# A fused attention and gated-feed-forward block: all q/k projections ahead of the gates, a planner that counts exponentials, maxima in steps of their own, even head sets

## The chip, the core and the metric

The kernel runs on one core of a Trainium2 chip. The core has a matrix engine (TensorE, PE), a vector engine (VectorE, DVE), an activation engine (ScalarE, ACT), a general engine (GpSimd, POOL), a queue that only issues transfers (SyncE, SP), and DMA engines between HBM and the on-chip memory. PE writes its results to the banks of PSUM, from which DVE and ACT read them. Each engine works through its own list of instructions in order; semaphores hold an instruction back until what it needs is there.

The metric is the device time of one launch in microseconds (us), the median of several runs. One launch was also recorded by the hardware profiler; the profile and the trace come from it.

## The reference

For `x` of 2048 rows and 576 columns (S = 2048, D = 576), 32 heads of width 18, and a feed-forward width of 4608:

```python
xn = layernorm(x)
q, k, v = split(xn @ wqkv)                       # 32 heads of width 18
p = softmax(q @ k.T * 18 ** -0.5)                # per head, 2048 x 2048
s = concat_heads(p @ v) @ wo
g = silu((gelu(xn @ w_gate) * (xn @ w_up)) @ w_down)
out = x + s * g
```

All data are float32. The kernel splits most operands into a high and a low float16 part and forms three products for one, so that the result stays near float32.

## The kernel before, in words

**Projections.** After the layer norm, the normalised rows stand transposed on the chip as a high and a low half (XHT, XL). The weights are taken in *units*: `v`, five *j units* (the q and k columns of one set of heads, `j0` to `j4`), eighteen *c units* (256 columns of `w_gate` and `w_up`, and the matching 256 rows of `w_down`), and `wo`. `prep` (L210) lays down what a unit's weights need: loads on SP's queue, maxima for a power-of-two scale, a round trip through HBM that spreads the maximum, then the split into a high half (ACT, L359) and a low half (POOL, L366 and L367, or one DVE instruction). These pieces wait in a background list, `bg`; `subtick` (L151) takes some of them when the room it is given allows it. `Rest` and `Gate` items hold the list back for a time or until a condition holds.

`v` and `j0` are projected near the start. The other 22 units form one stream, the **gate stream** (`order`, L1094 on; `pairs`, L1130 on). Its grain is a *pair*: 27 *slots* in two halves of 14 and 13, each slot two matmuls side by side on half the rows of the array (L517). A j unit has four pairs, a c unit eight; 4320 slots in all. Between the two halves of a pair, another product must have used PE (`g_run`, L1165). In the order before, the j units stand between the c units: j1, j2 (its pairs dealt out alternately with c0's), c1, c2, j3, c3, c4, j4, and then the rest.

A pair of a j unit is evacuated by ACT and DVE and stored to HBM (`evac_j`). A pair of a c unit goes through the gelu: evacuations on ACT, five products on POOL, a tanh on ACT, two more products on POOL, and a split into `hhi` and `hlo`. Two such pairs make a block, whose second half, when it is finished, queues eight *down stages* (`DownPair`, L792): the product with `w_down`, 12 matmuls a stage (L816). Every second stage is *late*: DVE then adds the result to `y` (L836).

**Attention.** Heads go in 16 *head pairs*. For a head pair, first the row maxima of the scores are needed: `qk1` (L1409) makes scores into one two-bank tile, and DVE reduces it (L1417). `max_end` (L1421) turns the 128 x 32 maxima into two rows that are appended to Q: a reduction (L1430), three POOL operations, a transpose (L1437), a DMA to HBM, and DMAs from there into QT (L1444). Then `qk2` (L1465) makes scores again, transposed and with the maximum taken off, ACT takes the exponential (L1475; L1477 and L1478 where the two heads lie in different sets, as each set has its own scale), and a *burst* multiplies three or four exponentials by V (L1494), which DVE adds up (L1502). `norm` divides and stores to OHL.

**The steps.** The main loop (from L1775 on) has 64 steps for each head pair. A step issues `qk2` for this head pair, `qk1` for the next one (from step 58 on, for the one after it), and then, as a plan says, a down stage or none and some slots of the gate stream. The last step of a gate pair holds the burst and no slots. The plan for one gate pair is made by `make_plan`: it tries all numbers of steps near a due size (`size`: steps left over pairs left) and all ways of putting down stages on them, spreads the slots by `spread`, and takes the layout with the least cost. The cost is the time that `lost` works out, plus terms for the distance from the due size and from the wanted number of down stages (`want`), plus others. A shortfall of down stages is carried into the next plan without a bound (`frac[1]`).

**Start and end.** Before the loop, 64 steps make the maxima of head pair 0 while `v` and then the gate stream fill PE (L1611 on); seven more steps then begin head pair 1. When the gate stream is over, the output products (`OutPair`) begin, which load OHL (`load_ohl`); the first call of that load stands in the step that finds the stream finished.

Of the kernel before, what the change touches and what calls it, by code (L numbers as in the profile page):

```python
# [24 lines left out]
NJ = 5  # L25
CF = 256
# [68 lines left out]
def kernel(ctx: ExitStack, tc: tile.TileContext, x, wqkv, wo, w_gate, w_up, w_down, out):  # L95
# [114 lines left out]
    def prep(name, parts, n, down=None, urgent=False, free=None, dfree=None, lead=1, vec=(), spare=False, early=False, slow=1.0):  # L210
# [139 lines left out]
        def split_hi(t):  # L350
            if t == 0:
                if spare == "P":
# [41 lines left out]
        act, dve = on_act(), on_dve()  # L394
        low_cost = [dve if t in vec else on_pool(2.75) for t in range(5)]
# [155 lines left out]
    def heads_of(j):  # L551
        return list(range(7 * j, min(7 * j + 7, H)))
# [72 lines left out]
    def spec_j(j):  # L625
        n = DH * len(heads_of(j))
        return f"j{j}", [(wqkv, 126 * j), (wqkv, D + 126 * j)], n
# [479 lines left out]
    def make_prep(i, **how):  # L1107
        kind, spec = order[i]
        w, pieces = prep(
            *spec, free=lambda: done_units[0] >= {2: 0, 3: 1}.get(i, i - 1),  # L1110
            dfree=lambda: kind[1] < 2 or dndone[kind[1] - 2] == NT,
            lead=1, vec=(1, 3) if i == 4 else (), **how,
        )
        preps[i] = w
        return pieces
# [14 lines left out]
    def pairs():  # L1130
# [5 lines left out]
        yield from unit(1)  # L1136
        ahead = [unit(2), unit(3)]
# [5 lines left out]
        for i in range(4, len(order) - 1):  # L1143
# [247 lines left out]
    def load_qk(p):  # L1391
        q = ap.tile([P, S], F16, tag="QT", name=f"QT{p}", bufs=3)
        k = ap.tile([P, S], F16, tag="KT", name=f"KT{p}", bufs=3)
        for h in range(2):
            j, hl = divmod(2 * p + h, 7)
# [25 lines left out]
    def max_end(p):  # L1421
# [3 lines left out]
        def a():  # L1425
            gp = nc.gpsimd
            defer.spend(on_pool(1.0))
            mx = sm.tile([P, 2, NT], F32, tag="rmx", name=f"rmx{p}", bufs=2)
            mc = st["mc"] = sm.tile([P, 2, 2, NT], F16, tag="rmc", name=f"rmc{p}", bufs=2)
            nc.vector.tensor_reduce(mx, PM[p], op=ALU.max, axis=AX.X, negate=True)  # L1430
# [9 lines left out]

        def c():
# [23 lines left out]
    def qk2(p, qb, kt, tag):  # L1465
# [7 lines left out]
        j0, j1 = (2 * p) // 7, (2 * p + 1) // 7  # L1473
# [123 lines left out]
    pj2, pc0 = make_prep(2, spare="P", early=True), make_prep(3, early=True, slow=1.5)  # L1597
    for p in (pj2, pc0):
        p.pop(0)[1]()

    def until_gate(p):
        n = next(k for k, f in enumerate(p) if isinstance(f, Gate))
        return p[:n], p[n:]

    pj2, sj2 = until_gate(pj2)
    pc0, sc0 = until_gate(pc0)
    bg.append(Rest(14.0))
    bg.extend(pj1 + pc0[:1] + pj2[:6] + pc0[2:10] + pj2[6:10] + pc0[11:12] + pj2[10:] + sj2 + pc0[13:] + sc0)
    fills(11, 2.0)
    k = 0  # L1610
    while k < 64:  # L1611
        if k == 12:
            load_qk(1)
        if done_units[0]:
# [4 lines left out]
            qk1(0, k)  # L1619
            subtick(FIRST)  # L1620
            g_run(7)
            subtick({"A": 0.75, "V": 0.3, "T": 0.5})
            k += 1
        else:
            qk1(0, k)
            qk1(0, k + 1)
            side = 0.0
            for _ in range(2):
                subtick(FIRST)
                side += FIRST["V"] - defer.room["V"]  # L1630
            fill(2.03 + side)
            k += 2
# [5 lines left out]
    for k in range(AHEAD + 1):  # L1638
# [4 lines left out]
        g_run(7)  # L1643
        subtick(dict(FIRST, T=1.75))
# [8 lines left out]
    ROW_MAX, EVAC, ADD, TOUCH = 1.28, 0.86, 0.75, 0.0  # L1653
# [22 lines left out]
    def lost(steps):  # L1676

        t = vec = red = 0.0
        ideal = 0.0
# [279 lines left out]
```

## Time and profile before

| | |
|---|---|
| median of 3 runs (lowest, highest) | 2538.12 us (2537.28, 2538.24) |
| the profiled execution | 2540.97 us |
| its span, first to last instruction | 2539.1 us |
| granted TensorE clock, mean | 0.998 |
| row maxima, L1417, DVE | 1250.9 us, 1024 of 1224 ns |
| exponentials, L1475, ACT | 995.2 us, 896 of 1112 ns |
| exponentials in halves, L1477 and L1478, ACT | 87.8 and 87.2 us, 128 of each |
| addition to `y`, L836, DVE | 219.8 us, 272 of 808 ns |

A row of the timeline reads: start in us from the beginning of the span, duration in us, engine, line of the kernel, operation, output <- inputs, shapes, how many of them, and in brackets how long the engine had been idle before and what ended that. A row of the windows has the stretch, its length, and for each engine the busy time in it with the number of instructions in brackets, then the granted clock, the DMA share and GB/s; when it is asked for one line, only that line's instructions are counted. A row of the groups has line, engine, operation, tiles, shapes and count, then busy us and the mean ns of one, then the idle time ahead of them. Times of one line on PE add up to more than its share, as neighbouring matmuls overlap.

### The profile page before, as it was taken

What the parts mean: (1) busy time and instruction counts of PE and PEld (TensorE: products, weight loads), DVE (VectorE), ACT (ScalarE), POOL (GpSimd) and SP (SyncE); (2) the same over time, 40 slices, a digit from 0 to 9 for tenths busy, and PEclk for the clock granted to TensorE, in tenths of its full rate; (3) what the DMA queues carried; (4) which work ended last, traced back from release to release, by engine and by line L of the source; (5) the groups of instructions that cost most, each with busy time, mean ns of one, the idle gap of its engine ahead of it and who ended that gap; (6) DMA issues with size and microseconds to landing.
All of it is one profiled execution on the core that took longest, in us unless ns stands there. A gap on an engine that the chain in (4) does not pass through costs nothing.

```text
span 2539.1 us, 61428 instructions
## 1 busy us (share of the span) xinstructions
PE 2490.0 (98%) x26216; PEld 1297.5 (51%) x26216; DVE 1837.8 (72%) x2108; ACT 1657.1 (65%) x2066; POOL 1542.0 (61%) x1587
## 2 busy tenths in 40 slices
PE   7999999999999999999999999999999999999898
PEld 6864544554445444445445444454444454544455
DVE  7587777787768777777777777776777777777444
ACT  6236676667776767666767676677766666666574
POOL 3367575547655476766757585857676767666413
PEclk9999999999999999999999999999999999999999
DMA  5631110221011210201111120101010111010124
GB/s 161 163 121 51 28 24 6 59 88 25 19 52 30 68 44 6 58 10 53 26 27 40 25 57 11 53 16 50 16 45 19 38 24 44 25 35 8 41 64 141
DMA packets 139689, 118.71 MB, mean 47 GB/s; under 512 B 64810, under 2 KB 118832, under 8 KB 139417
## 3 DMA queue, kind: packets, MB, share of 16 engines
q1 hardware_dynamic: 136553, 106.92, 15.4%
q0 software_dynamic: 1568, 5.37, 0.8%
q8 instruction: 206, 3.38, 0.6%
q10 hardware_dynamic: 1296, 2.51, 0.3%
q14 instruction: 66, 0.54, 0.1%
HBM read 84.89 MB, written 29.61 MB: 45 GB/s over the span
## 4 chain that ended last, share of the span: by engine, by line
PE 90%; DVE 5%; ACT 2%; DMA 1%; issue 1%; SPq 0%; POOL 0%; POOLq 0%; ACTq 0%; DVEq 0%
PE ma_t L517 17%; PE mb_t L517 16%; PE md_t L816 16%; PE md_t L1494 10%; PE s L1469 10%; PE s L1414 9%; PE ma_t L1494 8%; DVE PM L1417 1%; ACT P L1475 1%; PE md_t L998 1%; PE mb_t L998 1%; ACT P L1477 1%; PE pv_t L665 1%; PE ma_t L998 1%; PE ma_t L665 0%
## 5 line engine op out<-in xcount | busy, mean ns | idle before, releaser
L1417 DVE TENSOR_REDUCE PM<-s 128x2 f32<-128x1024 f32 x1024 | 1250.9, 1224 | 350.3 <-PE s L1414 343.2
L1475 ACT ACTIVATE P<-s,etab 128x1024 f32<-128x1024 f32 x896 | 995.2, 1112 | 590.3 <-PE s L1469 581.7
L517 PE MATMUL ma_t<-XHT,whi_c 64*128 64x512 f16 x1440 | 541.2, 376 | 0.5 <-DVE osb L1500 0.3
L517 PE MATMUL mb_t<-XHT,whi_c 64*128 64x512 f16 x1440 | 541.2, 376 | 0.2 <-ACT gv L722 0.2
L517 PE MATMUL ma_t<-XHT,wlo_c 64*128 64x512 f16 x1296 | 486.5, 375 | 0.0
L517 PE MATMUL mb_t<-XHT,wlo_c 64*128 64x512 f16 x1152 | 432.4, 375 | 0.0
L517 PE MATMUL ma_t<-XL,whi_c 64*128 64x512 f16 x1152 | 432.3, 375 | 0.0
L517 PE MATMUL mb_t<-XL,whi_c 64*128 64x512 f16 x1152 | 432.3, 375 | 0.0
L1469 PE MATMUL s<-QT,KT 56*128 56x512 f16 x2048 | 403.0, 380 | 4.4 <-DMA QT<-md 1.2
L1414 PE MATMUL s<-KT,QT 54*128 54x512 f16 x2048 | 396.7, 377 | 3.3 <-DVE PM L1417 2.6
L517 PEld LDWEIGHTS <-whi_c 64*128 64x128 f16 x5184 | 273.1, 94 | 216.6 <-issue 3.2
L816 PE MATMUL md_t<-dhi_c,hhi 64*128 64x288 f16 x2304 | 334.9, 283 | 1.9 <-DVE osb L1500 0.8
L816 PE MATMUL md_t<-dhi_c,hlo 64*128 64x288 f16 x2304 | 334.5, 283 | 0.0
L816 PE MATMUL md_t<-dlo_c,hhi 64*128 64x288 f16 x2304 | 334.1, 282 | 0.0
L752 POOL TENSOR_SCALAR tw<-tw 128x512 f32<-128x512 f32 x144 | 90.2, 626 | 376.2 <-ACT tw L744 376.1
L816 PEld LDWEIGHTS <-hhi 64*128 64x128 f16 x4608 | 237.7, 94 | 150.6 <-issue 10.7
L777 POOL TENSOR_TENSOR hlo<-gv,hhi 128x512 f16<-128x512 f32 x144 | 167.8, 1165 | 222.6 <-ACT hhi L770 219.7
L1494 PE MATMUL md_t<-P,VT 128*32 128x512 f32 x2296 | 267.2, 596 | 1.2 <-issue 0.9
L1469 PEld LDWEIGHTS <-KT 56*128 56x128 f16 x2048 | 123.8, 94 | 256.6 <-issue 166.9
L836 DVE SCALAR_TENSOR_TENSOR y<-md_t,c_c,y 128x576 f32<-128x576 f32 x272 | 219.8, 808 | 18.6 <-PE md_t L816 18.6
L1494 PE MATMUL ma_t<-P,VT 128*32 128x512 f32 x1712 | 200.2, 596 | 0.7 <-DVE ob L1040 0.4
L517 PEld LDWEIGHTS <-wlo_c 64*128 64x128 f16 x2592 | 136.7, 94 | 119.8
(255 smaller groups left out, 4062.0 us busy)
## 6 DMA issues: line engine op xcount, KB each, us to landing
draw_c<-in_B_w_down SPq DMA_DIRECT2D x18, 576.0 KB
raw_c<-in_B_w_gate SPq DMA_DIRECT2D x18, 512.0 KB
raw_c<-in_B_w_up SPq DMA_DIRECT2D x18, 512.0 KB
obr<-rd SPq DMA_DIRECT2D x30, 256.0 KB
KT<-KD SPq DMA_DIRECT2D x32, 224.0 KB
QT<-QD SPq DMA_DIRECT2D x32, 216.0 KB
VS<-vst POOLq DMA_DIRECT2D x16, 304.0 KB, 5.8
VT<-VS SPq DMA_DIRECT2D x16, 304.0 KB
```

The lines of the kernel that those rows point to most:

```text
L517: m = nc.tensor.matmul(o, lw, xx, start=self.stage == 0 and self.k == 0, stop=self.stage == 1 and self.k == self.slots - 1, skip_group_che ...
L665: self.last = nc.tensor.matmul(self.m[hf].t[:, 0:288], a, b, start=not second and k == 0, stop=bool(second) and k == n - 1, skip_group_che ...
L752: gp.tensor_scalar(st["t"], st["t"], 1.0, 1.0, op0=ALU.mult, op1=ALU.add)
L777: gp.tensor_tensor(hs.lo[:, ft], st["v"], hs.hi[:, ft], op=ALU.subtract)
L816: m = nc.tensor.matmul(self.t.t[:, hf, 0:288], a[r, ft, sl], b[r, ft, 288 * hf:288 * hf + 288], start=self.stage == 0 and k == 0, stop=sel ...
L836: nc.vector.scalar_tensor_tensor(yy, y, w.c, yy, op0=ALU.mult, op1=ALU.add)
L998: m = nc.tensor.matmul(o, a, b, start=self.stage == 0 and self.k == 0, stop=self.stage == 1 and self.k == len(terms) - 1, skip_group_check ...
L1414: nc.tensor.matmul(s1[:, h], QT[p][r, P * qt:P * qt + P], KT[p][r, 512 * kb:512 * kb + 512], start=True, stop=True)
L1417: nc.vector.tensor_reduce(PM[p][:, :, qt, kb:kb + 1], s1, op=ALU.max, axis=AX.X)
L1469: nc.tensor.matmul(s2[:, h], KT[p][r, P * kt:P * kt + P], QT[p][r, 512 * qb:512 * qb + 512], start=True, stop=True)
L1475: nc.scalar.activation(pt, s2, AF.Exp, scale=ETAB[j0])
L1494: nc.tensor.matmul(t.t[qd:qd + 32, :], VT[p][:, c0:c0 + 32], pt[:, h], start=kt == k0, stop=kt == k1, skip_group_check=True,)
```

## The change

Six things are done.

1. The head sets have 6, 6, 6, 7 and 7 heads (`HEADS`) where they had 7, 7, 7, 7 and 4.
2. In the gate stream all j units stand ahead of the c units; j4's pairs are dealt out alternately with c0's. The preparation of j2, j3, j4 and c0 is put into the background list before the start, in a new order by hand. `home` says where a unit's split weights live: those of j2 and j3 take buffers of the exponentials ("P").
3. In the start, the number of slots in a step follows a target (`g_round`): 540 slots by the end of it.
4. `lost` works with a chain for each of PE, DVE and ACT: the row maximum, the exponential (1.113, or 1.4 where a head pair straddles sets), the late evacuation.
5. `make_plan` wants at least four down stages in a pair, weighs the distance from the wanted number and from the due size more, bounds what is carried over, and improves the twelve best layouts by moving single slots inside a half.
6. `max_end` forms the two parts of the maximum by two DVE operations in place of three on POOL, and its three parts are issued ahead of steps 58, 59 and 60; before, the first came behind step 57 and the others behind step 60.

```diff
+HEADS = [0, 6, 12, 18, 25, 32]
...
     def heads_of(j):
-        return list(range(7 * j, min(7 * j + 7, H)))
+        return list(range(HEADS[j], HEADS[j + 1]))
...
-    for k, j in enumerate(units_j):
-        order += [j] + [units_c.pop(0) for _ in range((0, 3, 2, 2)[k])]
-    order += units_c
+    order += units_j + units_c
...
-            *spec, free=lambda: done_units[0] >= {2: 0, 3: 1}.get(i, i - 1),
+            *spec, free=lambda: done_units[0] >= {2: 0, 3: 0, 4: 1, 5: 2}.get(i, i - 1),
...
         def a():
-            gp = nc.gpsimd
-            defer.spend(on_pool(1.0))
-            mx = sm.tile([P, 2, NT], F32, tag="rmx", name=f"rmx{p}", bufs=2)
+            mx = st["mx"] = sm.tile([P, 2, NT], F32, tag="rmx", name=f"rmx{p}", bufs=2)
+            nc.vector.tensor_reduce(mx, PM[p], op=ALU.max, axis=AX.X, negate=True)
+
+        def b():
+            mx = st["mx"]
             mc = st["mc"] = sm.tile([P, 2, 2, NT], F16, tag="rmc", name=f"rmc{p}", bufs=2)
-            nc.vector.tensor_reduce(mx, PM[p], op=ALU.max, axis=AX.X, negate=True)
-            gp.tensor_scalar(mx, mx, 2.0 ** -15, None, op0=ALU.mult)
-            gp.tensor_scalar(mc[:, :, 0], mx, 1.0, None, op0=ALU.mult)
-            gp.tensor_tensor(mc[:, :, 1], mx, mc[:, :, 0], op=ALU.subtract)
-
-        def b():
+            nc.vector.tensor_scalar(mc[:, :, 0], mx, 2.0 ** -15, None, op0=ALU.mult)
+            nc.vector.scalar_tensor_tensor(
+                mc[:, :, 1], mx, 2.0 ** -15, mc[:, :, 0], op0=ALU.mult, op1=ALU.subtract
+            )
+
+        def c():
             st["mt"] = sm.tile([P, 64], F16, tag="rms", name=f"rms{p}", bufs=1)
             nc.vector.transpose(st["mt"], st["mc"].rearrange("p a b c -> p (a b c)"))
             st["md"] = dp.tile([P, 64], F16, tag="md", name=f"md{p}", bufs=2)
             nc.sync.dma_start(st["md"], st["mt"])
-
-        def c():
             md = st["md"]
...
+    pj2, pj3, pj4 = (make_prep(k, spare="P", home="P" if k < 4 else None, early=True) for k in (2, 3, 4))
+    pc0 = make_prep(5, early=True)
...
+    bg.extend(pj1 + pc0[:1] + [lj3] + pj2[:8] + pj3[:6] + pj2[9:13] + pj3[7:8] + pj2[13:])
+    bg.extend([lj4] + pj3[9:] + pj4[:6] + pc0[2:5] + pj4[7:8] + pc0[5:9] + pj4[9:13] + pc0[9:10])
+    bg.extend(pj4[13:19] + pc0[11:12] + pj4[19:] + [Rest(2.5)] + pc0[13:])
...
+    START = 20 * 27
+
+    def g_round(target):
+        n = g_left()
+        if gs.all - gs.left + n > target + 4:
+            n = (n + 1) // 2
+        room = 0.75 if n < 10 else 1.5
+        subtick({"A": room, "V": room, "T": 0.12 + 0.1 * n})
+        g_run(n)
+        subtick({"A": room, "V": 0.3, "T": 0.1 + 0.1 * n})
...
-            subtick(FIRST)
-            g_run(7)
-            subtick({"A": 0.75, "V": 0.3, "T": 0.5})
-            k += 1
+            g_round(START * (k + 1 - k0) / (70 - k0))
...
+    def lost(steps, exp):
+
+        t = ideal = ex = red = y = 0.0
+        vec = 0.83
         for d, g, late, first in steps:
-            t1 = max(t + 0.21, red + 0.055)
-            e1 = t1 + 0.22
-            vec = red = max(vec, e1 + 0.16) + ROW_MAX - 0.05
-            w = d * D_STAGE + (BURST if g is None else g * G_SLOT)
+            q = max(t, ex + 0.055)
+            t1 = max(q + 0.22, red + 0.055)
+            ex = max(ex - 0.1, q + 0.48) + exp
+            vec = red = max(vec - 0.085, t1 + 0.42) + 1.226
+            t = t1 + 0.21
             if d:
-                vec = max(vec, e1 + D_STAGE) + (EVAC if late else TOUCH)
-            t = e1 + w
-            if g is None:
-                vec = max(vec, t) + ADD
-            elif first:
-                vec = max(vec, t) + TOUCH
-            ideal += BLOCK + w
-        return max(t, red + 0.055 - 0.21) - ideal
+                t = (t if late else max(t, y + 0.055)) + D_STAGE
+                if late:
+                    vec = y = max(vec - 0.085, t + 0.1) + 0.808
+            t += BURST if g is None else g * G_SLOT
+            ideal += BLOCK + d * D_STAGE + (BURST if g is None else g * G_SLOT)
+        return max(t, red + 0.055 - 0.22, ex + 0.055) - ideal
...
-        want = min(8.0, dleft[0] / pairs + frac[1])
+        want = min(8.0, max(4.0, (dleft[0] - 16) / pairs) + frac[1])
...
-                    cost = lost(seq) + busy * ds[-1] + held_a * (not ds[0]) + 0.3 * abs(n - size) + 0.15 * abs(sum(ds) - want) + 0.02 * (max(works) - min(works))
+                    fixed = busy * ds[-1] + held_a * (not ds[0]) + 0.3 * abs(n - size) + 0.15 * (n - size) ** 2 + 0.25 * abs(sum(ds) - want)
+                    found.append((lost(seq, exp) + fixed + 0.02 * (max(works) - min(works)), fixed, seq, m))
...
-        frac[1] = want - sum(d for d, _, _, _ in seq)
+        frac[1] = max(-0.3, min(0.3, want - sum(d for d, _, _, _ in seq)))
...
+            if more and 0 <= i - 64 + AHEAD < 3:
+                if i == 64 - AHEAD:
+                    steps = max_end(p + 1)
+                steps[i - 64 + AHEAD]()
...
-            if more and i == 60:
-                steps[1]()
-                steps[2]()
-            if more and i == 57:
-                steps = max_end(p + 1)
-                steps[0]()
```

More of the change, by code (lines that the diff above doesn't have):

```diff
@@ L208, with prep @@
         pass
-    def prep(name, parts, n, down=None, urgent=False, free=None, dfree=None, lead=1, vec=(), spare=False, early=False, slow=1.0):
+    def prep(name, parts, n, down=None, urgent=False, free=None, dfree=None, lead=1, vec=(), spare=False, home=None, early=False, slow=1.0):
         w = W()
@@ L392, in rest @@
                 pieces.append(Rest(span))
-        act, dve = on_act(), on_dve()
-        low_cost = [dve if t in vec else on_pool(2.75) for t in range(5)]
+        act, dve = on_act(), on_dve(0.7 if n > P else 0.42)
+        low_cost = [dve if t in vec else on_pool(2.75 if n > P else 1.65) for t in range(5)]
         if not early:
@@ L551, in heads_of, with set_of @@
     def heads_of(j):
-        return list(range(7 * j, min(7 * j + 7, H)))
+        return list(range(HEADS[j], HEADS[j + 1]))
+    def set_of(h):
+        j = max(j for j in range(NJ) if HEADS[j] <= h)
+        return j, h - HEADS[j]
     jdone = {}
@@ L1134, in unit @@
             done_units[0] += 1
-        yield from unit(1)
-        ahead = [unit(2), unit(3)]
+        for i in range(1, NJ - 1):
+            yield from unit(i)
+        ahead = [unit(NJ - 1), unit(NJ)]
         yield next(ahead[0])
@@ L1142, in pairs @@
         yield from ahead[1]
-        for i in range(4, len(order) - 1):
+        for i in range(NJ + 1, len(order) - 1):
             yield from unit(i)
@@ L1613 @@
             load_qk(1)
+        qk1(0, k)
         if done_units[0]:
@@ L1618 @@
                 banks.remove(("mc", "pv"))
-            qk1(0, k)
-            subtick(FIRST)
-            g_run(7)
-            subtick({"A": 0.75, "V": 0.3, "T": 0.5})
-            k += 1
-        else:
[L1625 to L1632, printed above, removed]
+            g_round(START * (k + 1 - k0) / (70 - k0))
+        else:
+            subtick({"A": 0.9, "V": 0.9, "T": 2.1})
+            fill(1.9)
+            k0 = k + 1
+        k += 1
     load_v(0)
```

59 lines of the change are left out of this document (35 added, 24 removed).

## The prediction

> **What bounds the kernel now.** I read the page's busy times first, then the timeline of the TensorE (PE), then windows of single lines, then the waits of VectorE (DVE), and the end of the run last.
>
> ```profile
> PE 2490.0 (98%) x26216; PEld 1297.5 (51%) x26216; DVE 1837.8 (72%) x2108; ACT 1657.1 (65%) x2066; POOL 1542.0 (61%) x1587
> ```
>
> PE has work at 98% of the span and no other engine is over 72%. But a matmul's row is longer than the distance to the next one, so short stalls do not show as idle time. I therefore price PE's work by the distances between starts, where nothing waits:
>
> ```profile
> 1011.73 0.38 PE L517 MATMUL mb_t<-XHT,whi_c 64*128 64x512 f16 x1
> ...
> 1013.24 0.40 PE L1469 MATMUL s<-QT,KT 56*128 56x512 f16 x2
> ...
> 1013.78 2.78 PE L1494 MATMUL md_t<-P,VT 128*32 128x512 f32 x24
> 1016.50 0.39 PE L1469 MATMUL s<-QT,KT 56*128 56x512 f16 x2
> ...
> 1016.94 0.38 PE L517 MATMUL ma_t<-XHT,whi_c 64*128 64x512 f16 x1
> ...
> 1017.81 0.28 PE L816 MATMUL md_t<-dhi_c,hhi 64*128 64x288 f16 x2
> ...
> 1018.54 0.38 PE L1469 MATMUL s<-QT,KT 56*128 56x512 f16 x2
> ```
>
> Seven gate slots (two L517 matmuls each) take 1.51 us, so 0.2157 a slot; a burst of 24 L1494 matmuls 2.72; the two score products of a step 0.44 (1016.50 to 1016.94); a down stage (twelve L816 matmuls) 0.73. Ahead of the burst, 1013.24 + 0.44 leaves 0.10 idle. These are the counts of the main loop, for L517, L816, L1494, L1414 and L1469 in this order:
>
> ```profile
> 207.00:2386.60 2179.60, 1001.19 (x7992) 422.15 (x7992) 1.00 0.13 34
> ...
> 207.00:2386.60 2179.60, 505.67 (x6720) 342.06 (x6720) 1.00 0.13 34
> ...
> 207.00:2386.60 2179.60, 441.26 (x3824) 112.28 (x3824) 1.00 0.13 34
> ...
> 207.00:2386.60 2179.60, 369.55 (x1908) 123.58 (x1908) 1.00 0.13 34
> ...
> 207.00:2386.60 2179.60, 373.20 (x1914) 115.26 (x1914) 1.00 0.13 34
> ```
>
> 3996 slots x 0.2157 = 862; 560 stages x 0.73 = 409; 3824/24 x 2.72 = 433; 3822/4 x 0.44 = 420. Together 2124 of 2179.6: **the loop loses some 55 us**, and no rearrangement of it can win more. Where it loses them, a step poor in work shows, on PE and on DVE:
>
> ```profile
> 1007.79 0.39 PE L1469 MATMUL s<-QT,KT 56*128 56x512 f16 x2
> ...
> 1009.45 0.39 PE L1469 MATMUL s<-QT,KT 56*128 56x512 f16 x2
> ```
>
> ```profile
> 1008.50 1.23 DVE L1417 TENSOR_REDUCE PM<-s 128x2 f32<-128x1024 f32 x1 [0.48 <-PE s L1414]
> 1010.21 1.23 DVE L1417 TENSOR_REDUCE PM<-s 128x2 f32<-128x1024 f32 x1 [0.48 <-PE s L1414]
> ```
>
> The step holds five slots and no down stage: 0.44 + 1.08 = 1.52 of work in 1.66. The scores for the next maxima have one bank, so the round is a reduction, 1.23, and 0.48 until new scores stand: 1.71. A step with less work than that stalls. Steps are starved because the planner bunches the down stages. L816 in four neighbouring gate pairs, two early and two late:
>
> ```profile
> 384.37:398.58 14.21, 3.59 (x48) 2.35 (x48) 1.00 0.06 13
> 398.58:413.42 14.84, 3.62 (x48) 2.52 (x48) 1.00 0.03 6
> 1034.21:1046.61 12.40, 0.90 (x12) 0.58 (x12) 1.00 0.18 62
> 1046.61:1063.47 16.86, 6.30 (x84) 4.25 (x84) 1.00 0.04 10
> ```
>
> Each couple is 13 steps, 54 slots, 8 stages and two bursts of 24: 11.65 + 5.84 + 5.72 + 5.44 = 28.65. Dealt four and four it takes 29.05 and loses 0.40; dealt one and seven it takes 29.26 and loses 0.61. Pairs with no down stage are worst:
>
> ```profile
> 873.38 0.39 PE L1469 MATMUL s<-QT,KT 56*128 56x512 f16 x2
> ...
> 885.52 0.39 PE L1469 MATMUL s<-QT,KT 56*128 56x512 f16 x2
> ```
>
> 12.14 for 27 slots, six steps and a burst, 11.18 of work: 0.96 lost. Some 148 pairs run in the loop; six like this cost 6 us, the other 142 at about 0.28 some 40, and about 9 is left for isolated stalls and for the two head pairs whose heads lie in different sets.
>
> **The change part by part.** *The plan.* The start is to do 540 slots, where 4320 - 3996 = 324 are done now. So 216 x 0.2157 = 47 us of PE work moves out of the loop into the start, at no gain by itself: PE is the bound in both. What stays is 3780 slots, 140 pairs, all of gates, over 960 steps: 6.86 steps a pair, about 120 pairs of seven steps and 20 of six, with four stages each. The early couple above gives both prices as the old planner laid them out: six steps, 14.21 - (5.82 + 2.92 + 2.64 + 2.72) = 0.11; seven steps, 14.84 - 14.54 = 0.30.
>
> ```profile
> 402.45 0.38 PE L1469 MATMUL s<-QT,KT 56*128 56x512 f16 x2
> ...
> 404.44 0.40 PE L1469 MATMUL s<-QT,KT 56*128 56x512 f16 x2
> ```
>
> At these rows the loop would lose 120 x 0.30 + 20 x 0.11 = 38. If nothing but the 0.10 ahead of a burst were left it would be 14. The new cost function charges the row maximum, the exponential and the late evacuation each to its engine, and a search moves single slots, so between 0.30 and 0.10 I take 0.18 for a seven, a little nearer to the lower end, as the one wait of the early seven (1.99 between the rows above, where 0.44 + 0.73 + 0.65 of work stood, behind an evacuation on DVE) is of the kind now charged: 120 x 0.18 + 20 x 0.11 = 24. Of the 9 us of isolated stalls 6 remain: 30 in all, **a gain of 25**, with ends at 55 - 20 = 35 and 55 - 47 = 8.
>
> *Even head counts.* Where a head pair straddles two sets, two exponentials run for one:
>
> ```profile
> L1475 ACT ACTIVATE P<-s,etab 128x1024 f32<-128x1024 f32 x896 | 995.2, 1112 | 590.3 <-PE s L1469 581.7 <-PE s L1414 4.3 <-PE md_t L998 1.0
> ...
> L1477 ACT ACTIVATE P<-s,etab 128x512 f32<-128x512 f32 x128 | 87.8, 686 | 76.2 <-PE s L1469 74.4 <-PE s L1414 1.5
> ```
>
> With sets of 6, 6, 6, 7, 7 only pair 12 does, where pairs 3 and 10 did. 64 steps get one exponential of 1.11 back for two of 0.69: 0.26 us each on ScalarE (ACT), 17 us in all, of which PE sees only what falls in steps that wait for ACT; it is within the 3 us of isolated stalls just taken.
>
> *Maxima in steps of their own.* Three small GpSimd (POOL) operations go, two on DVE come, and the reduction, the split and the transpose are put ahead of steps 58, 59 and 60.
>
> ```profile
> L1556 DVE TENSOR_TENSOR onl<-osb,onh 128x512 f16<-128x512 f32 x32 | 27.8, 868 | 0.0
> ...
> L1430 DVE TENSOR_REDUCE rmx<-PM 128x32 f32<-128x128 f32 x16 | 4.4, 278 | 0.1
> ```
>
> ```profile
> 2364.32 0.68 DVE L1556 TENSOR_TENSOR onl<-osb,onh 128x512 f16<-128x512 f32 x1
> ```
>
> The trace shows neither new operation. By the nearest row (0.28, a reduction over four times the elements) two of them cost at most 0.56 a head pair, 9 us of DVE in all; by the slack of a step with 2 us of work against 1.71 they cost nothing. I take nothing: they are spread over steps of their own, and what queues behind them is the next row maximum, 0.3 early. If the cover is gone it is up to 9 us.
>
> Against this part speaks the Trainium skill, "SBUF — State Buffer", section "Who interferes with whom": a VectorE instruction with two SBUF inputs and a GpSimd instruction that reads SBUF lock each other out for a whole instruction. The row of L1556, such an instruction, agrees in kind: its mean is 868 ns where the undisturbed one at 2364.32 took 0.68. By the rule each of the two new operations could wait for the rest of a POOL operation; that is rival 3.
>
> *The end of the loop.* There PE waits once for long:
>
> ```profile
> 2386.78 0.69 DVE L1502 TENSOR_TENSOR osb<-md_t,osb 128x512 f32<-128x512 f32 x1 [5.96 <-PE md_t L1494]
> ...
> 2387.39 0.24 DVE L1437 STREAM_TRANSPOSE rms<-rmc 128x64 f16<-128x64 f16 x1
> ...
> 2390.50 1.15 SPq L931 DMA_DIRECT2D ohl<-OHL  x2
> ...
> 2395.06 0.42 PE L998 MATMUL ma_t<-whi_wo,ohl 64*128 64x288 f16 x1 [8.02 <-DMA ohl<-OHL]
> ...
> 2396.23 0.45 PE L816 MATMUL md_t<-dhi_c,hhi 64*128 64x288 f16 x2
> ...
> 2397.67 0.64 PE L1469 MATMUL s<-QT,KT 56*128 56x512 f16 x2
> ...
> 2400.74 0.52 PE L1469 MATMUL s<-QT,KT 56*128 56x512 f16 x2
> ```
>
> The first output product waits 8.0 us for its operand. Its load stands on SP's queue behind the DMA of the maxima, that behind a transpose, and that on DVE behind the addition of a burst. From the transpose to the landed operand it is 7.7 us. After it PE runs at half speed (1.44 for a stage that costs 0.73) until about 2400.74: half of 5.7, 2.8 us more. In the changed kernel the transpose stands ahead of step 60, so ahead of a burst in that step: earlier by that burst, 2.72, and about a step, 1.7. And the terms that hold a pair to its due size are stronger, so the last pair should end nearer to step 960 than now and the output product start later. I take about 5 us of the stall and the 2.8 of slow clock to go: **a gain of 8**, with ends at 0 and 11. Stages left to the end cost what they cost in the loop.
>
> *The start.* It becomes longer by the 47 us counted above. Five weights must be split there before their units begin, the first gates' last:
>
> ```profile
> L366 POOL TENSOR_SCALAR raw_c<-raw_c,s_c 128x512 f32<-128x512 f32 x88 | 139.6, 1586 | 5.3 <-ACT whi_c L359 5.3
> L367 POOL TENSOR_TENSOR wlo_c<-raw_c,whi_c 128x512 f16<-128x512 f32 x88 | 102.4, 1164 | 7.3
> ```
>
> ```profile
> 207.06 0.84 PE L1469 MATMUL s<-QT,KT 56*128 56x512 f16 x2 [1.19 <-DMA QT<-md]
> ```
>
> The gates' split is five times 2.75 = 13.75 us of POOL; the background list puts it after the fourth q/k weights. The q/k units give it 12 pairs of 5.8 us and more to hide in, and the gates' units of POOL work (gelu) do not run meanwhile, so I take it as hidden; uncovered it is 14 us at most. Three queues carry what is moved. SP gets the stores of twelve more q/k pairs into the start, six a pair: at 0.57 each (the OHL issue above, 1.15 for two) 3.5 us in a pair of 5.8, so they fit. The load of the fourth set's weights takes the buffer of the second's, and SP stands at it until POOL has split those, five times 2.75 at most by the wider rows; behind it are the stores of the first units, which no one reads before the loop. ACT and DVE get two evacuations each a pair instead of gelu work. The wait of 1.19 for the first maxima should go, since three longer steps follow their DMA: **a gain of 1**, with ends at -14 and +4.
>
> **Sum.** 25 + 8 + 1 = 34 us. The profiled execution took 2540.97, 1.9 of it around the span, so it would come to 2507; it lies 2.85 above the median of the runs, 2538.12, on which I put the prediction: **2504**.
>
> **The rivals.** (1) *The tail keeps its stall*: the last pair ends as early as now, and the operand's load is late again. For it speaks that the load is still issued only once the gate stream is over, in the very step that may use it. 2538 - 25 - 1 = 2512. (2) *The deal does not do what it says*: stages come in lots of eight, as a gate block's second half is finished, and with seven steps a pair the old couple's 0.30 stays or is passed; the loop gains 8 and the tail 5. 2525. Against it speaks the early couple, which deals four and four with lots of eight. (3) *The maxima on DVE block*. Fifteen head pairs times one POOL operation of 1.16 (L367) are 17 us, less the 2 us that meet slack: 2538 - 34 + 15 = 2519. For it speaks the spread of L1556, against it that most steps have slack. (4) *Slower: starved steps.* Taking slots out of the loop leaves 3.94 a step for 4.16. If seven-step pairs stall like pairs without downs, halfway between 0.30 and 0.96, it is 140 x 0.63 = 88, with 6 of isolated stalls 94 against 55: 2538 + 39 - 9 = 2568. It decides from (55 + 9 - 6)/140 = 0.41 a pair on.
>
> **How the numbers follow.** Forecast 0.56 (2504, by itself 2490 to 2516); rival 1 0.16; rival 2 0.12; rival 3 0.07; rival 4 0.09. A measurement of this kernel tells about 0.2%, 5 us, from no change. Of rival 2 and 3 about 0.05 falls within that, so faster 0.86, same 0.05, slower 0.09. The range goes from the far ends of loop and tail together with the start's (35 + 11 + 4 = 50: 2488, and 4 less for the rounding of the prices) to 2532, which takes in rivals 1 to 3 and leaves out the slower one.
>
> **What would show it.** Right: L816 counts near 48 in every pair of the loop, seven steps to most pairs; fewer steps of five slots without a stage; the loop's loss, by the same prices, near 30; the row maximum's idle time in front of it smaller in sum; no 8 us wait ahead of the first L998 and a granted clock of 1.00 around it; L1477 x64. Wrong: windows of L816 that still alternate between 84 and 12; waits of L1417 or of the reduction's successors on POOL at steps 58 to 60; a gap of PE before the first gates' units in the start; pairs of seven steps that lose over 0.41.

## The result, and the profile after

| | before | after |
|---|---|---|
| median of 6 runs each (lowest, highest) | 2538.01 us (2536.41, 2540.53) | 2554.75 us (2553.26, 2558.73) |
| ratio to before, 95% interval | | 1.0068 [1.0055, 1.0081] |
| the profiled execution, its span | 2540.97, 2539.1 us | 2558.73, 2556.9 us |
| granted TensorE clock, mean | 0.998 | 0.993 |

The change made the kernel slower by 17 us where 34 us less were forecast. The prediction priced PE's work by distances between starts; the same prices, laid on every run of matmuls in both traces, give the time lost in each stage. *Start* is from the first product of `v` to the first transposed scores (`qk2`), *loop* from there to the last gate slot, *tail* the rest. The prices are taken here to more digits than the prediction prints; with the printed ones the losses of the loop come out 2 to 4 us lower, in all kernels alike to some 1 us, so differences of less than that are not read:

| us, length / lost | start | loop | tail |
|---|---|---|---|
| before | 147.1 / 9.1 | 2175.0 / 57.4 | 157.0 / 34.5 |
| after | 221.8 / 34.1 | 2134.1 / 64.7 | 141.1 / 21.0 |

The tail gained 13.5 us, the start lost 25, the loop lost 7 more instead of 25 less. These are three groups of the page of the kernel after (busy us and mean ns, then idle time ahead and what ended it); L1418 and L1498 are `qk1` and the burst, L1421 the row maximum, L841 the addition to `y`:

```profile
L1421 DVE TENSOR_REDUCE PM<-s 128x2 f32<-128x1024 f32 x1024 | 1251.7, 1223 | 350.1 <-PE s L1418 332.9
...
L1498 PE MATMUL md_t<-P,VT 128*32 128x512 f32 x3744 | 434.7, 596 | 26.4 <-DVE y L841 22.6
...
L1418 PE MATMUL s<-KT,QT 54*128 54x512 f16 x2048 | 394.4, 378 | 23.0 <-DVE PM L1421 23.0
```

Two waits stand out. **The burst waits for the addition to `y`** (L841), which it hardly did before. And `qk1` waits 23 us for the row maximum, 17 of it in the start.

First the loop. Windows of the down stages' line alone, over four neighbouring gate pairs of after, in the same layout as those shown of before:

```profile
901.60:916.55 14.95, 3.59 (x48) 2.29 (x48) 1.00 0.22 73
916.55:932.35 15.80, 3.59 (x48) 2.30 (x48) 1.00 0.00 1
932.35:947.08 14.73, 3.60 (x48) 2.34 (x48) 1.00 0.02 3
947.08:962.89 15.81, 3.59 (x48) 2.30 (x48) 1.00 0.43 84
```

The deal is done: four stages (48 matmuls) in each pair, as in all pairs of the loop but two, and 122 of 140 pairs have seven steps. The 124 steps of five slots without a stage, which lost 20 us before, are gone. But a pair now ends like this (timeline of after, DVE and then PE):

```profile
912.97 0.81 DVE L841 SCALAR_TENSOR_TENSOR y<-md_t,c_c,y 128x576 f32<-128x576 f32 x1
913.70 1.22 DVE L1421 TENSOR_REDUCE PM<-s 128x2 f32<-128x1024 f32 x1
```

```profile
913.01 0.38 PE L1473 MATMUL s<-QT,KT 56*128 56x512 f16 x2
...
913.83 2.78 PE L1498 MATMUL md_t<-P,VT 128*32 128x512 f32 x24 [0.23 <-DVE y L841]
```

The two score products cost 0.44, so the burst could follow at 913.45 and, with the 0.10 that it always loses, at 913.55. It begins at 913.83, 0.05 behind the end of L841 (913.78). A burst in a step without a stage writes the bank `md`, the same in which the late stage of the step before still waits to be read. In after all bursts of the loop but one stand in such a step. Of these 138, 104 begin 0.38 to 0.41 late and the others 0.09 to 0.18. Together that is 45 us of the loop's 64.7, 0.32 on the mean; the 0.36 in the expectation of e1_charge counts in the wait shown next. Before, there were 89 such bursts, at about 0.11.

One more wait in the loop is of another kind. It comes once, inside a burst (timeline of after, PE and then SP):

```profile
1281.90 1.92 PE L1498 MATMUL md_t<-P,VT 128*32 128x512 f32 x16 [0.23 <-DVE y L841]
1287.97 1.27 PE L1498 MATMUL ma_t<-P,VT 128*32 128x512 f32 x8 [4.14 <-DMA VT<-VS]
```

```profile
1273.56 0.45 SPq L243 DMA_DIRECT2D raw_c<-in_B_w_gate  x1
...
1279.16 0.67 SPq L1410 DMA_DIRECT2D VT<-VS  x1
```

The last eight matmuls of the burst wait for a load of V, which SP issued behind the five loads of a gate unit's weights. With the slow clock behind it (0.79 from 1290 to 1295) this costs some 6 us, nearly all that the loop lost more than before. No run moved this load by itself.

Now the start. SP's queue and the waits of ACT, DVE and PE that follow, from the timeline of after:

```profile
217.31 0.42 SPq L243 DMA_DIRECT2D raw_c<-in_B_w_gate  x1
...
220.84 2.68 SPq L259 DMA_DIRECT2D draw_c<-in_B_w_down  x1
223.62 0.82 SPq L588 DMA_DIRECT2D KD<-evh  x1
```

```profile
232.70 0.60 ACT L568 ACTIVATE evh<-pv_t 126x512 f16<-126x512 f32 x1 [10.44 <-DMA KD<-evh]
```

```profile
233.33 0.69 DVE L573 SCALAR_TENSOR_TENSOR evl<-pv_t,evh 126x512 f16<-126x512 f32 x1 [10.35 <-ACT evh L568]
233.94 3.48 DVE L1421 TENSOR_REDUCE PM<-s 128x2 f32<-128x1024 f32 x3
```

```profile
235.21 0.61 PE L1418 MATMUL s<-KT,QT 54*128 54x512 f16 x2 [10.12 <-DVE PM L1421]
```

Read it upwards. PE waits for a row maximum; that stands on DVE behind the low half of a q/k unit; that waits for the high half on ACT; and ACT waits for a *store*: `evh`, the high half on its way to HBM, has three buffers, and one is free only when the DMA that stores it has read it. SP issued these stores from 223.62 on, behind the five loads of c1's weights, and the first has landed by 232.7.

### The profile page after: what moved, and what is told of

It reads as the page before. It is cut to its first block, busy times and chain, and to the rows that moved or that the text cites. A ratio compares the mean times of both kernels' runs of the same rounds, so it can differ in the third digit from the quotient of the medians.

```text
span 2556.9 us, 61384 instructions
## 1 busy us (share of the span) xinstructions
PE 2474.2 (97%) x26216; PEld 1305.8 (51%) x26216; DVE 1839.1 (72%) x2134; ACT 1651.4 (65%) x2002; POOL 1534.2 (60%) x1543
## 4 chain that ended last, share of the span: by engine, by line
PE 82%; DVE 12%; DMA 3%; issue 1%; POOL 1%; ACT 1%; SPq 0%; ACTq 0%; POOLq 0%; DVEq 0%
PE ma_t L518 17%; PE md_t L1498 17%; PE mb_t L518 14%; PE md_t L821 13%; PE s L1473 8%; PE s L1418 8%; DVE PM L1421 6%; DVE y L841 3%; PE ma_t L1498 1%; DMA KD<-evh 1%; DMA VT<-VS 1%; PE pv_t L518 1%; PE md_t L1003 1%; PE mb_t L1003 1%; PE ma_t L1003 1%
## 5 line engine op out<-in xcount | busy, mean ns | idle before, releaser
L1421 DVE TENSOR_REDUCE PM<-s 128x2 f32<-128x1024 f32 x1024 | 1251.7, 1223 | 350.1 <-PE s L1418 332.9
L1479 ACT ACTIVATE P<-s,etab 128x1024 f32<-128x1024 f32 x960 | 1067.6, 1114 | 591.9 <-PE s L1473 582.7
L1498 PE MATMUL md_t<-P,VT 128*32 128x512 f32 x3744 | 434.7, 596 | 26.4 <-DVE y L841 22.6
L1418 PE MATMUL s<-KT,QT 54*128 54x512 f16 x2048 | 394.4, 378 | 23.0 <-DVE PM L1421 23.0
L1473 PE MATMUL s<-QT,KT 56*128 56x512 f16 x2048 | 396.4, 379 | 0.5 <-ACT P L1479 0.4
L518 PEld LDWEIGHTS <-whi_c 64*128 64x128 f16 x5184 | 261.0, 94 | 243.4 <-issue 7.2
L821 PEld LDWEIGHTS <-hhi 64*128 64x128 f16 x4608 | 228.4, 94 | 133.2 <-issue 4.1
L1498 PEld LDWEIGHTS md_t<-P,VT 128*32 128x32 f32 x3744 | 107.6, 109 | 279.7 <-issue 194.9
L1506 DVE TENSOR_TENSOR osb<-md_t,osb 128x512 f32<-128x512 f32 x138 | 95.4, 691 | 206.4 <-PE md_t L1498 206.1
L841 DVE SCALAR_TENSOR_TENSOR y<-md_t,c_c,y 128x576 f32<-128x576 f32 x272 | 219.9, 809 | 15.0 <-PE md_t L821 15.0
```

Of the source, the lines that this page charges most:

```text
L518: m = nc.tensor.matmul(o, lw, xx, start=self.stage == 0 and self.k == 0, stop=self.stage == 1 and self.k == self.slots - 1, skip_group_che ...
L821: m = nc.tensor.matmul(self.t.t[:, hf, 0:288], a[r, ft, sl], b[r, ft, 288 * hf:288 * hf + 288], start=self.stage == 0 and k == 0, stop=sel ...
L841: nc.vector.scalar_tensor_tensor(yy, y, w.c, yy, op0=ALU.mult, op1=ALU.add)
L1418: nc.tensor.matmul(s1[:, h], QT[p][r, P * qt:P * qt + P], KT[p][r, 512 * kb:512 * kb + 512], start=True, stop=True)
L1421: nc.vector.tensor_reduce(PM[p][:, :, qt, kb:kb + 1], s1, op=ALU.max, axis=AX.X)
L1473: nc.tensor.matmul(s2[:, h], KT[p][r, P * kt:P * kt + P], QT[p][r, 512 * qb:512 * qb + 512], start=True, stop=True)
```

## The experiments

Each expectation was on record before its run. All runs were timed beside the kernel before, whose median was between 2539.4 and 2540.6 in these batches.

**e1_charge.** After, with one more line in `lost`: a burst without a stage ahead of it in its step also waits for the bank of `y`.

```diff
+            if g is None and not d:
+                t = max(t, y + 0.055)
             if d:
                 t = (t if late else max(t, y + 0.055)) + D_STAGE
```

> The changed kernel with one line more in the planner's cost function: a burst in a step without a down stage starts no earlier than the late evacuation to y has left its bank. Theory (the burst waits for the bank md, which the last late stage of its pair still holds): the planner moves that stage ahead, the gap ahead of bursts falls from about 0.36 to 0.11 us in most of the 138 pairs, the loop loses some 30 to 35 us where it loses 65 now, and the time falls by 25 to 34 us, to 2521 to 2530. Rival (the gap is the array's switch from score products to the burst, or the exponentials come late): layouts change, but the gap stays near 0.36 and the time within 6 us of 2555.

2519.52 us, 0.992 [0.9904, 0.9937], 1.5 below the range expected. The planner now ends a pair of seven with a step of six slots, and the late stage stands a step earlier. The pair that took 14.95 takes 14.65. Its end in the timeline of e1_charge, and the group of the burst on its page:

```profile
902.35 0.38 PE L1473 MATMUL s<-QT,KT 56*128 56x512 f16 x2
902.88 2.78 PE L1498 MATMUL md_t<-P,VT 128*32 128x512 f32 x24
```

```profile
L1498 PE MATMUL md_t<-P,VT 128*32 128x512 f32 x3744 | 434.7, 596 | 2.8 <-DVE ob L1038 2.3
```

0.53 from scores to burst instead of 0.82. The bursts begin 0.09 late on the mean, 13 us in all where it was 45, and the wait for V does not occur in these layouts. So the loop loses 26.5 us instead of 64.7, of which some 32 are the line's own doing and 6 came along by chance; the start is as it was (33.0).

**e2_c1late.** After, with c1's preparation, its loads among it, held until the last q/k unit is done.

```diff
         if i < len(order) and i not in preps:
+            if order[i][0] == ("c", 1):
+                bg.append(Gate(lambda: done_units[0] >= NJ))
             bg.extend(make_prep(i))
```

> The changed kernel, but the preparation of c1, with its load of 1.9 MB, does not begin before the units of q and k are done. Theory (that load fills the DMA engines just when the q/k stores are to read the evacuation buffers, of which there are three; ACT waits for a buffer, DVE for ACT, the row maxima for DVE, PE for the maxima): the wait of 10.1 us at 225 and the half speed of PE behind it go, the start loses some 18 us where it loses 34, and the time falls by 10 to 17 us. Rival (SP's issue of the stores alone is the limit, or the weights are not ready): under 4 us of gain.

2560.86 us, 1.0082 [1.0067, 1.0097]: a miss in the time, 6 us above after. The start lost 17.6 instead of 34.1, as expected, but the loop lost 82.7. What the start gained came back as another wait, which with the slow clock behind it costs 16 us between 319 and 341; these are two of PE's rows of this run:

```profile
325.62 0.61 PE L518 MATMUL ma_t<-XHT,wlo_c 64*128 64x512 f16 x1 [5.42 <-POOL wlo_c L368]
...
330.34 0.60 PE L518 MATMUL ma_t<-XHT,wlo_c 64*128 64x512 f16 x1 [3.25 <-POOL wlo_c L368]
```

The load, now issued at 257 us, was too late for the split of c1's own weights: their maxima stood between the loop's work on DVE until 296 us, and POOL began the split at 322.76.

**e5_cst.** After, with the constant rows of K for sets 1 to 4 (`KD<-cst`, 16 DMAs) written ahead of the start and not as each set begins.

> The changed kernel, but the constant rows of K for sets 1 to 4, four DMAs a set and 3 us of SP's queue each, are written before the start and no longer ahead of each unit's stores. Theory (stores are held up by what stands ahead of them on SP): the waits at 158 to 170, 6 us with the half speed behind them, go; the time falls by 4 to 9 us. Rival (only the load of c1 matters): within 3 us of the changed kernel's 2555.

2561.59 us, 1.0088 [1.0073, 1.0103]: a miss. SP's row of this run says why:

```profile
89.69 17.20 SPq L613 DMA_DIRECT2D KD<-cst  x16
```

SP is held 17.2 us, and the loads of the fourth set's weights (j3) stand behind it; DVE then waits 11.36 us at their first maximum and PE 8.47 in the `v` stage.

**e3_plan_only.** The kernel before with the new `lost`, `spread` and `make_plan`; order, start, sets and maxima as before.

> The kernel before with the new planner alone (make_plan, lost, the search), everything else as before. If the plan is what loses in the loop, bursts behind a late evacuation appear here too: pairs with four stages, a gap of about 0.36 ahead of bursts, the loop near 57 us of loss as before (starved steps go, slower bursts come), and the time within 8 us of 2538. If the loss of the changed kernel's loop came from the order of the units or from the maxima, the loop here loses only 30 and the time is near 2510.

2521.31 us, 0.9931 [0.9914, 0.9947], between the two cases expected. The planner alone is worth 18 us: the tail loses 21.0 instead of 34.5, the loop 49.5 instead of 57.4, though 33.4 of these are lost at bursts.

**e6_oldstart and e7_oldstart_all.** The kernel before with the new planner and the charge of e1_charge (e6); the same with the even sets and the maxima on DVE too (e7), which is all of the change but the order of the units and its start, with the line of e1_charge.

> The kernel before with the new planner and with the charge for the bank of y on the burst (the edit of e1_charge); the order of the units, the start, the sets of seven heads and the maxima on POOL stay as before. By the theory that the change lost time in two places of its own, the burst's wait in the loop and the stores in the start, both are gone here: the start of e3_plan_only lost 8.5 us against 33.0 of e1_charge, and its 145 bursts lost 33.4 us in all, 0.23 each, against 0.095 in e1_charge, so that some 19 us of its 2521.3 go: 2499 to 2506, below e1_charge (2519.5) by 13 to 20. By the rival that the order of the units has to be all q and k first for the loop to be even (with the old order pairs of five and six steps remain), the loop keeps 10 us or more of that: 2510 to 2520.

> As e6_oldstart, with the even sets of heads and the maxima in steps of their own too: all of the change but the order of the units and the start that goes with it. Beside e1_charge it undoes that one part: by the theory that the order costs 20 to 25 us in the start and brings less than 5 in the loop, 2497 to 2508; by the rival that the order also brings the loop what the start loses, 2515 to 2523. Beside e6_oldstart it shows what the even sets and the maxima are worth: the prediction had 0 to 3 us for the two, so -3 to +3.

2500.67 us, 0.9846 [0.983, 0.9863], and 2506.72 us, 0.9869 [0.9854, 0.9883]. Both lie in the ranges of their theories, but e7 is 6 us above e6 where at most 3 were expected; the runs of the maxima below take this up. Without the new order the start loses 8.6 and 10.3. The loop keeps 32.4 and 38.3, more than the 26.5 of e1_charge: eight pairs of five and six steps without stages remain, which lose some 7 us in either.

**e8_c1mid.** e1_charge, with the gate of e2_c1late opened earlier:

```diff
+                bg.append(Gate(lambda: jdone.get(NJ - 1, 0) >= 6))
```

> e1_charge with the loads of the second gate unit's weights held until six of the eight stores of the last q and k set are issued (about 238 us), instead of 217 us (e1_charge) or 257 us (e2_c1late). e2_c1late took 16.5 us from the start, but its weights then came late and PE stood 10.0 and 3.3 us at them at 320 to 336 us. By the theory that the stores standing behind this load in the DMA queues are what stops PE for 10 us at 224, and that the weights need their load by about 240, both are mostly gone: 2504 to 2511. By the rival that the two waits are one amount of work for POOL, ACT and DVE that comes back wherever it is pushed, 2516 to 2523.

2501.75 us, 0.9848 [0.9833, 0.9863], 17.8 below e1_charge, so the rival that the wait comes back wherever the load is pushed falls. By the traces the start gives 13 of it and the loop 3. Windows of after (first fence) and of e8_c1mid (second), with the busy time of PE, PEld, DVE, ACT and POOL, then clock, DMA share and GB/s:

```profile
218.00:224.00 6.00, 6.00 (x58) 3.85 (x56) 2.26 (x3) 0.60 (x1) 0.00 (x0) 1.00 0.71 215
224.00:230.00 6.00, 1.09 (x11) 0.47 (x7) 0.00 (x0) 0.00 (x0) 0.00 (x0) 0.76 0.62 206
230.00:236.00 6.00, 0.79 (x4) 0.34 (x5) 2.67 (x3) 0.60 (x1) 0.00 (x0) 0.50 0.41 132
236.00:250.00 14.00, 14.00 (x110) 8.09 (x108) 9.05 (x11) 4.78 (x7) 6.56 (x7) 0.83 0.08 26
```

```profile
218.00:224.00 6.00, 5.96 (x56) 3.70 (x53) 2.97 (x4) 1.19 (x2) 0.00 (x0) 1.00 0.46 148
224.00:230.00 6.00, 5.55 (x52) 3.47 (x53) 3.89 (x4) 2.23 (x3) 1.40 (x2) 1.00 0.36 123
```

PE works through the stretch in which it stood, and the clock stays at 1.00 there. The start loses 20.0, the loop 23.5, and no wait for c1's weights is left.

**e10_c0late.** e8_c1mid, with c0's loads put behind those of the third and fourth q/k set, for the wait left in the `v` stage.

> e8_c1mid with the loads of the first gate unit's weights put behind those of the third and the fourth q and k set (some 15 to 25 us later than at 81 us). In the start of e8_c1mid DVE stood 8.36 us at the first maximum of the fourth set's weights, whose load came behind the 1.8 MB of the gate unit's, and PE 5.47 us for DVE at 111.6 us. By the theory that this wait is the order of the loads, those 4 to 6 us go: 2495 to 2499. By the rival that the v stage has no time to spare for three sets of maxima, or that the gate unit's weights come late in their turn, 2500 to 2508.

2503.95 us, 0.9859 [0.9844, 0.9874]: a miss. The wait moved: DVE stands 8.87 us at the spread of a maximum (`mb_j`, to 117.2 us), a load that SP issued at 107.4, just ahead of c0's, and PE 5.66 behind DVE. What is left of the start, some 11 us against the old order, was not settled.

**e9_heads_max, e11_max_pool, e12_heads, e13_pool_steps.** The even sets and the maxima, taken apart. Both were put into the kernel before (e9); the old maxima were put back into e8_c1mid (e11); the even sets alone were put into e6_oldstart (e12); and e13 is e12 with the maxima at the new places but on POOL. The core of e13's edit, against e7_oldstart_all:

```diff
-            nc.vector.tensor_scalar(mc[:, :, 0], mx, 2.0 ** -15, None, op0=ALU.mult)
-            nc.vector.scalar_tensor_tensor(
-                mc[:, :, 1], mx, 2.0 ** -15, mc[:, :, 0], op0=ALU.mult, op1=ALU.subtract
-            )
+            gp.tensor_scalar(mx, mx, 2.0 ** -15, None, op0=ALU.mult)
+            gp.tensor_scalar(mc[:, :, 0], mx, 1.0, None, op0=ALU.mult)
+            gp.tensor_tensor(mc[:, :, 1], mx, mc[:, :, 0], op=ALU.subtract)
```

> The kernel before with the even sets of heads and the maxima in steps of their own on DVE, and nothing else: old planner, order and start. The prediction set 0 (at most 9 lost) for the maxima and up to 3 gained for the sets: 2536 to 2541. By the rival that the three DVE steps block the evacuations ahead of a burst, 2545 or more.

> e8_c1mid with the maxima as before the change (one reduction on DVE and three small steps on POOL at the 57th half step, transpose and the DMAs at the 60th), the even sets and the new order kept. e9_heads_max stood 4 us above before and e7_oldstart_all 6 us above e6_oldstart. By the theory that the maxima on DVE cost this (two instructions of 128x32 took up to 1.2 us each on DVE, and the row maxima stand behind them), 2496 to 2499. By the rival that the even sets cost it, since an odd set boundary inside a head pair is not what the loop waits for, 2500 to 2504.

> e6_oldstart with the even sets of heads alone added, the maxima left on POOL: what lies between e6_oldstart (2500.7) and e7_oldstart_all (2506.7). By the theory that the maxima on DVE cost the 6 us, 2498 to 2502; by the rival that the even sets cost them, 2504 to 2508.

> e12_heads with the maxima in steps of their own at the places that the change gives them (three steps from half step 64 less the lead), but with the small steps on POOL as before instead of DVE: between e12_heads (2493.9) and e7_oldstart_all (2506.7), which differ by engine and place together. In e7_oldstart_all the 128x32 steps on DVE took 0.17 and 0.19 us where POOL was idle and ended 0.04 us behind POOL's own instruction where it wasn't, up to 1.2 us. By the theory that the engine is the cost, 2492 to 2498; by the rival that the place is (the transpose and its DMAs some steps elsewhere, or the reduction ahead of another evacuation), 2501 to 2508.

| | us | ratio, interval |
|---|---|---|
| e9_heads_max | 2544.51 | 1.0014 [1.0005, 1.0024] |
| e11_max_pool | 2498.35 | 0.9836 [0.9821, 0.985] |
| e12_heads | 2493.90 | 0.9819 [0.9802, 0.9835] |
| e13_pool_steps | 2501.45 | 0.9852 [0.9835, 0.9868] |

The maxima as the change has them cost 3.4 us in the new order (e8 less e11) and 12.8 in the old (e7 less e12); of the latter the place has 7.5 (e13 less e12) and the engine 5.3 (e7 less e13). These are differences of medians of four runs each, some from different batches, and the runs of one kernel spread by up to 3 us; that both have a part is shown, how large each is only roughly. The time of e13 lies at the near end of the range of the place, so that theory fits better, though not alone. e12 itself came 4 us below its range, and e9 half a microsecond below that of its rival. Part of the place shows: in the start, where the three parts are issued two steps apart, the transpose now stands in the third part instead of the second, and the first scores of the loop wait longer for the maxima. From the timelines of e12_heads and, in the second fence, e13_pool_steps:

```profile
205.14 0.83 PE L1474 MATMUL s<-QT,KT 56*128 56x512 f16 x2 [0.92 <-DMA QT<-md]
```

```profile
205.48 1.31 PE L1475 MATMUL s<-QT,KT 56*128 56x512 f16 x2 [3.70 <-DMA QT<-md]
```

With the slow clock behind it, the start loses 0.8 more and the loop's first two steps 2.5 more; the other 4 us of the place were not traced to a wait.

The even sets gained 6.8 (e6 less e12). **e12_heads is the fastest version**, 1.8% below before: the new planner with the charge, and the even sets, in the old order with the old start and the old maxima.

## Why the prediction was wrong, step by step

*The bound.* PE was the bound, and the slots moved into the start cost nothing by themselves: the start's length less what it lost grew by 49.7 us (187.7 against 138.0), where 47 were counted (230 slots were moved, not 216), and the loop's fell by 48.

*The plan: the step that failed first.* The prediction took 0.18 for a pair of seven steps "as the one wait of the early seven ... is of the kind now charged". It is charged only where the next stage waits for the bank of `y`, not where a burst does, and the pairs the search liked best ended in just that. A seven lost 0.49 (0.44 without the one wait for V) and the loop 64.7, where 0.18 and 30 were forecast: 45 of it ahead of bursts, some 6 at the wait for V, which no term of the sum had. With the missing line (e1_charge) a seven loses 0.19 and the loop 26.5: the size was right for a planner that charges every user of the bank. The line was to be seen in the diff: the charge stands under `if d`.

*Rival 4* set 0.41 a pair as the point from which the change is slower, and the loop of after came to 64.7 / 140 = 0.46. But its mechanism is not what ran: 211 steps of seven slots without a stage lost 0.013 each.

*The start: the second.* The stores of the first units stood behind a load, and the prediction wrote that "no one reads [them] before the loop". No one reads what they write; but ACT needs the buffers that they read. The start lost 25 us more where a gain of 1, at worst a loss of 14, was forecast. About half of it is this stall and the slow clock behind it: e8_c1mid, which moves only c1's loads by 22 us, takes back 13 in the start, 17.8 in all by the medians. e7_oldstart_all shows that the other 11 too come with the order or its start; their cause stays open. The load named was not the costly one either. SP did stand at it (j4's), from 125 to 132 us, while POOL split the weights of j2; ACT then waited 3.26 us for a store at 141, but PE nowhere more than 0.4 before 163. In e1_charge the same stand reached PE, with 3.6 us at 145.8. The 10 us came from c1's loads.

Those two steps carry the miss: with both mended (e8_c1mid) the kernel comes to 2501.75, against 2504 forecast; the rest of the start's loss, 11 us, and what loop and tail gained beyond the forecast offset each other. That the two times lie so close is luck.

*The end of the loop.* Right, and undersized: the 8.0 us wait is gone (1.34 ahead of the first output product, timeline of after below), and the tail lost 13.5 less, where 8, at most 11, was forecast. The planner alone does all of it (e3_plan_only, 21.0); the maxima and the even sets without it do 5.6 (e9_heads_max, 28.9). Of the two reasons given, the second was enough.

```profile
2422.25 0.29 PE L1003 MATMUL ma_t<-whi_wo,ohl 64*128 64x288 f16 x1 [1.34 <-DMA ohl<-OHL]
```

*The maxima.* Taken at nothing, at most 9 us. They cost 3.4 in the order of the change and 12.8 in the old. Rival 3 was a real mechanism, as the last section shows; here the maxima cost a quarter of its 15 us, the new place of the steps included.

*The even sets.* Set within 3 us of isolated stalls, they brought 6.8 in the old order. The split exponentials fell to x64 as forecast, but are not shown to be the cause: of the 4.9 us that the loop lost less, 2.7 lie where head pair 3 runs and next to none where pair 10 does, and the waits that went are single ones of `qk1` for the row maximum.

## What to carry to other kernels

When a planner's cost function charges a wait, list every instruction that can wait for the same buffer: the search will move the wait to the one left out. A store that nobody reads for long is still urgent if its source buffer is to be refilled, so it should not be queued behind bulk loads, and neither should a load that is needed soon, as that of V in the loop; and a load moved out of the way must be watched at its own consumer, or the wait only changes place. Take a change of many parts apart in both orders: here a planner that gains 18 us by itself, and 40 with one line more, was hidden under an order that lost 25 in the start.

## What the runs showed of the hardware

Two VectorE instructions of 32 elements a partition took from 0.17 to 1.21 us, by what GpSimd did. The lines view of e7_oldstart_all (min, median, max in ns), and one head pair's turn on DVE and on POOL:

```profile
L1437 DVE TENSOR_SCALAR rmc<-rmx x16: 170/246/987, 195.0 to 2360.1; 128x32 f16<-128x32 f32 x16
L1438 DVE SCALAR_TENSOR_TENSOR rmc<-rmx,rmc x16: 191/194/1205, 195.2 to 2360.3; 128x32 f16<-128x32 f32 x16
```

```profile
491.62 0.29 DVE L1437 TENSOR_SCALAR rmc<-rmx 128x32 f16<-128x32 f32 x1
491.95 1.21 DVE L1438 SCALAR_TENSOR_TENSOR rmc<-rmx,rmc 128x32 f16<-128x32 f32 x1
493.08 1.21 DVE L1422 TENSOR_REDUCE PM<-s 128x2 f32<-128x1024 f32 x1
```

```profile
490.60 1.27 POOL L742 TENSOR_TENSOR tw<-tw,gs 128x512 f32<-128x512 f32 x1
491.84 1.26 POOL L743 TENSOR_TENSOR gv<-gv,gs 128x512 f32<-128x512 f32 x1
```

Each ends 0.04 to 0.06 us behind the POOL instruction that was running (491.87, 493.10) and the row maximum stands behind them; where POOL was idle, as at 773.11 and 773.31, they took 0.17 and 0.19. The Trainium skill, "SBUF — State Buffer", section "Who interferes with whom", has it that a VectorE instruction with two SBUF inputs, or one in a two-port mode, which `tensor_scalar` can enter, and a GpSimd instruction that reads SBUF keep each other out for a whole instruction. These rows agree for both forms; that the one with a single input ran in such a mode, no run here shows. Not every GpSimd instruction had this effect: beside L367, a `tensor_scalar` on POOL, L1438 took 0.19 (1926.34).

PE's stall of 10 us in the start cost more than its length: in the windows of after shown above the granted clock fell to 0.50 while PE stood, and was 0.83 in the 14 us from 236 on, in which it worked again.
